# One of VectorE's shifted arrays moved in halves to GpSimd in an attention-plus-feed-forward kernel

## The chip, the cores and the metric

The kernel runs on one core of a Trainium2 chip. The time is the device time of one execution in microseconds (us). The kernel before took 769.64 us, the median of three runs (769.48 to 770.63). The engines of the core are TensorE (PE in the profile), VectorE (DVE), ScalarE (ACT), GpSimd (POOL) and SyncE (SP, which here only issues transfers).

## The reference

For one sequence of 2048 rows and 512 columns, attention with 32 heads of 16 columns and a gated feed-forward block of width 1792 are computed from the same x, and mixed by a gate per row.

```python
qkv = (x @ wqkv).reshape(B, S, 3, H, Dh).transpose(2, 0, 3, 1, 4)     # H = 32, Dh = 16
scores = einsum("bhqd,bhkd->bhqk", q, k) * Dh ** -0.5
a = (softmax(scores) @ v).transpose(0, 2, 1, 3).reshape(B, S, D) @ wo
b = (silu(x @ w_gate) * (x @ w_up)) @ w_down
g = sigmoid((x * gate_w).sum(-1))
out = g * a + (1 - g) * b
```

The exponentials are the large part: 32 heads x 2048 x 2048 of them.

## The kernel before, in words

The attention is cut into 32 units: a block of 512 queries (four of them) and a group of four heads (eight of them). A unit has 16 key tiles of 128 keys. A key tile of a unit, called n in the code, is four blocks of 128 keys x 512 queries, one per head. TensorE computes a block of scores into PSUM, something takes the exponential of it into SBUF, and TensorE multiplies it with the values into `o_ps`, where a unit's 16 key tiles are summed. `pv` (line 902) emits that product: one call is a "piece" of four matmuls, one per head, which run side by side on the 32-column groups of the array.

Exponentials are taken in two ways.

- **On ScalarE.** `emit_pair` (line 704) computes two blocks into `s_t` (two buffers), and one `Exp` over 128x1024 writes `e_t`. A key tile takes two of them, and then one piece of `pv`.
- **On VectorE.** `emit_d` (line 774) computes a single block into `d_t` (one of three PSUM banks). VectorE reads it out of PSUM with a multiply and an add into 16-bit integers, which read as bfloat16 are a rough power of two. Four such reads fill one array of 128x2048, called y, for the whole key tile. Then the rough exponential is mended in one of two ways, picked per key tile by `quad` (line 1469) and kept in `groups`:
  - `groups[n] == 4`: three arrays more, each y plus a constant (`copy`, line 817, `SHIFTS` 25, 56 and 94). All four go to TensorE, which adds them up: four pieces of `pv`.
  - `groups[n] == 2`: two arrays of y's bits (`bits`, line 825) and a product of y with one of them (`product`, line 834): two pieces of `pv`.

The arrays live in seven homes of 128x2048 (`home`, line 762), of which the seventh lies in `wd_t` or `kaug`.

Nothing is ordered by the hardware's own choice. The program is written in one pass, and a planner decides in Python, while the kernel is built, what each engine does next. `Plan` (line 289) has a clock for TensorE, ScalarE and VectorE, and each emitted instruction moves its engine's clock by a cost that is written in the code: 0.6 for a read of PSUM or a 128x2048 shift on VectorE, `MUL_US` 1.135 for the product, `ACT_US` 0.9167 for an exponential, 0.217 for a piece. The instructions of an engine are chained in that order by `ordered` (line 152), so the order is fixed once the kernel is built; the hardware adds only the waits.

What the change touches:

- `fill_dve` (line 854) writes VectorE's instructions as long as VectorE's clock is behind TensorE's. It chooses between `vops` (shifts, bits and products that wait for their turn), `d_wait` (reads of `d_t` that are due) and `owed` (all other VectorE work, with due times, put there by `later`, line 309).
- `m_free` (line 361) says when one of the three banks is free again: VectorE's clock plus 0.2. `emit_d` says when a `d_t` can be read: TensorE's clock plus 0.28 (line 807).
- `v_unit` (line 1444) decides whether VectorE may take one more key tile from ScalarE, from the work that it has already and from the clocks. So a lighter VectorE takes more key tiles.
- `quad` picks the form with four pieces when few homes are free or when TensorE has had idle time to spare (`spare`), or when `EAGER` says so. Before, `EAGER` is always false.

The feed-forward block's matmuls (`gu`, `ops`, `dps`) and the projections are cut into pieces too and laid by a pacer between the attention's. GpSimd writes constants in the first 12 us and does nothing after. A helper records each operation, so the profile shows most VectorE work under line 176, ScalarE's under 167 and matmuls under 164; the tiles' names tell them apart.

Of the kernel before, what the change touches and what calls it, by code (L numbers as in the profile page):

```python
# [79 lines left out]
def kernel(  # L80
# [37 lines left out]
    NV = 4  # L118
# [58 lines left out]

    vec = Ordered(nc.vector)
    queue = Ordered(nc.sync)


    xT = big.tile([P, DC, S], BF16, name="xT")
# [104 lines left out]


    class Plan:
        pe = dve = act = 0.0  # L290
        mode = last = None
        seq = 0
        slot = -1
# [8 lines left out]
    def spend(mode, mms, ready=0.0):  # L302
# [3 lines left out]
        plan.pe = max(plan.pe + (FLIP if mode != plan.mode else 0.0), ready) + (0.226 if mode == "F" else 0.217) * mms  # L306
        plan.mode = mode

    def later(cost, f, ready=None, key=None):
# [13 lines left out]

    def pay(i=0):
        ready, cost, f, c, key = owed.pop(i)
        spend_v(cost, ready, key)
# [33 lines left out]

    def m_free(ps, t):
        i = [h is ps for h in held].index(True)
        banks[i], held[i] = t + 0.2, None

    def emit_piece(c):
        mms, f = c.pieces[c.i][:2]
# [407 lines left out]
    def emit_d(i, rows=32, riding=False):  # L774
        if not vcur:
            n = v_take()
            waiting[n] = [NV, None, take_home()]
            vcur.update(n=n, left=list(range(NV)), y=None)
            y_live[0] += 1
        n, left, cur = vcur["n"], vcur["left"], waiting[vcur["n"]]  # L780
        left.remove(i)
        end = []
        d_t = m_tile("d_t", end if riding else None)
        score(d_t[:, :], 4 * n + i, rows)
        if not left:
            vcur.clear()

        def first():
            if cur[1] is None:
                cur[1] = home(*cur[2])  # L790
            h, y = cur[1]
            vec.tensor_scalar(out=y[:, i * QBW:(i + 1) * QBW], in0=d_t[:, :], scalar1=EXP_A, scalar2=EXP_B[groups[n]],
                              op0=ALU.mult, op1=ALU.add)
            m_free(d_t, plan.dve)
            cur[0] -= 1
            if cur[0]:
                return
# [12 lines left out]
    copies = {}  # L810
    part = {}

    def ready(n, k, h, c):
        copies[n, k] = (c.bitcast(BF16), h)
        vready.append((plan.dve + 0.3, n, k))

    def copy(n, k, i, y):
        h, c = home()
        vec.tensor_scalar(out=c, in0=y, scalar1=SHIFTS[k - 1], scalar2=None, op0=ALU.add)
        ready(n, k, h, c)  # L820
        if k == 3:
            drop(i, plan.dve + 0.2)
            y_live[0] -= 1

    def bits(n, k, y):
        h, c = home()
# [21 lines left out]

    def pay_v():
        cost, f, key, _, _ = vops.pop(0)  # L850
        spend_v(cost, 0.0, key)
        f()

    def fill_dve():

        while plan.dve <= plan.pe + 0.2:
            now = plan.dve
            due = [k for k, o in enumerate(owed) if o[0] <= now + 0.05]
            free = [k for k in due if owed[k][4] is None or owed[k][4] != plan.last]
            fit = bool(vops) and vops[0][3] // KT <= closed + AHEAD and c_ready() <= now  # L860
            if fit and vops[0][3] // KT < au and vops[0][2] != plan.last:
                pay_v()
            elif d_wait and d_wait[0][2] // KT < au and d_wait[0][0] <= now + 0.05:
                pay_d()
            elif free:
                pay(free[0])
            elif d_wait and d_wait[0][0] <= now + 0.05:
                pay_d()
            elif fit and vops[0][2] != plan.last:
                pay_v()  # L870
            elif due:
                pay(due[0])
            elif fit:
                pay_v()
            elif d_wait or owed or vops and vops[0][3] // KT <= closed + AHEAD:
                t = min([w[0] for w in d_wait] + [o[0] for o in owed[:1]]
                        + [c_ready()] * bool(vops and vops[0][3] // KT <= closed + AHEAD))
                if t > plan.pe:
                    break
                plan.dve = max(plan.dve, t)  # L880
                plan.last = None
            else:
                break
# [18 lines left out]
    def pv(n, k=None, most=QBW):  # L902

        un = n // KT
        c0 = cut.pop("done", 0)
        c1 = min(QBW, c0 + most)
        cols = slice(c0, c1)
        if un not in o_of:
            while un and un - 1 not in osbs:
                pay()  # L910
            plan.pe = max(plan.pe, o_end[0])
            o_of[un] = ps_o.tile([P, QBW], F32, tag="o", name="o_ps")
        if v_of(n) is not None:
# [12 lines left out]
        share = (c1 - c0) / QBW  # L926
        if c1 < QBW:
            cut.update(item=(n,) if k is None else (n, k), done=c1)
            spend("C", share, 0.0 if k is not None else max(e_end[b] for b in range(4 * n, 4 * n + 4)))
# [11 lines left out]
        spend("C", share, 0.0 if k is not None else max(e_end.pop(b, 0.0) for b in range(4 * n, 4 * n + 4)))  # L941
# [192 lines left out]

    plan.act = plan.pe
    plan.dve = plan.pe + 3.9


    pace = Pacer()
# [277 lines left out]
    def next_pv():  # L1417
        flush_act()
        while not pv_list(None):
            if d_wait:  # L1420
                pay_d()
            elif vops and c_ready() < 1e9:
                pay_v()
            elif owed:
                pay()
            else:
                lone_d()
        emit_pv(pv_list(None)[0])
# [45 lines left out]
            return False  # L1474
        return True
    FREE4 = 2
    EAGER = lambda q, b: False
    GQL = lambda: []
    back = [0]

    def want_d():
# [60 lines left out]
        at_ += not half  # L1542
        forward()
    flush_act()
    while closed < UNITS or vops or vcur:
        fill_dve()
        while owed and owed[0][0] <= plan.pe:
            pay()
        if plan.slot < SLOTS + 1:
            begin(plan.slot + 1)  # L1550
            pace.credit = max(pace.credit, 2.0)
        if vcur:
            lone_d()
            continue
        c = side(2.0)
        if not pv_list(plan.pe) and c is not None:
            put_piece(c)
            continue
        if closed == UNITS - 1 and pv_left(closed) <= 2 and not a_ps[2:]:
            tail_ready()  # L1560
            tail(3)
        next_pv()
# [6 lines left out]
            f()  # L1569
    while owed:  # L1570
        pay()
    assert not vops and not vready and not vcur and not d_wait and not copies and au == closed == UNITS


    assert not at
# [59 lines left out]
```

## Time and profile before

| what | value |
|---|---|
| median of three runs | 769.64 us (769.48 to 770.63) |
| the profiled execution | 769.63 us, of which its span is 767.9 us and 1.73 us lie around it |
| granted TensorE clock | 1.000 |
| busy: TensorE, VectorE, ScalarE, GpSimd | 733.1, 738.8, 752.5, 10.6 us |
| exponentials on ScalarE | 780, 728.3 us busy |
| key tiles on VectorE | 122 of 512: 44 with four pieces, 78 with two |

How to read it: the span runs from the first to the last instruction of that execution. Busy time is the union of an engine's instructions, so instructions that overlap on one engine count once; their mean duration can be longer than the distance from one start to the next. The last row is from the order of instructions in the built program: 488 blocks `d_t`, 288 shifts or bits over 128x2048, 78 products over 128x2048.

### The profile page before, as it was taken

To read this page: it belongs to the slowest core of one execution; us is meant where nothing else is said; L and a number is where in the kernel's file an instruction comes from. 1 tells how busy PE (TensorE), PEld (TensorE's weight loads), DVE (VectorE), ACT (ScalarE), POOL (GpSimd) and SP (SyncE) were. 2 spreads that over 40 slices of the span, in tenths; PEclk is the share of its full clock that TensorE was granted. 3 is DMA by queue.
4 is the path that set the end of the run, shared out by engine and by line. 5 is a ranking of instruction groups with operands and counts; after the bars stand their busy time and mean duration, and the time that the engine had idled before them with its cause. 6 is when DMAs were issued, how large, how long until landed. Compare 5 with 4: busy or idle time off the path is not lost.

```text
span 767.9 us, 22047 instructions
## 1 busy us (share of the span) xinstructions
PE 733.1 (95%) x9044; PEld 221.6 (29%) x9045; DVE 738.8 (96%) x1213; ACT 752.5 (98%) x849; POOL 10.6 (1%) x25
## 2 busy tenths in 40 slices
PE   8999999999999999999999999999999999999997
PEld 3323222222222222223322222223222322222222
DVE  6889999999999999999999999999999999999994
ACT  5999999999999999999999999999999999999996
POOL 5000000000000000000000000000000000000000
PEclk9999999999999999999999999999999999999999
DMA  8002304134200113220100230311000232100001
GB/s 192 2 5 50 73 15 85 31 107 101 57 19 13 32 24 78 60 52 22 37 26 12 49 84 20 75 34 41 20 12 26 60 77 59 31 16 16 16 28 35
DMA packets 91020, 34.38 MB, mean 45 GB/s; under 512 B 75488, under 2 KB 90472, under 8 KB 90920
## 3 DMA queue, kind: packets, MB, share of 16 engines
q1 hardware_dynamic: 89192, 32.66, 17.8%
q8 instruction: 70, 1.15, 0.6%
q10 hardware_dynamic: 1728, 0.33, 0.2%
q14 instruction: 30, 0.25, 0.1%
HBM read 21.55 MB, written 2.35 MB: 31 GB/s over the span
## 4 chain that ended last, share of the span: by engine, by line
ACT 32%; PE 30%; DVE 28%; issue 8%; DMA 1%; SPq 1%; DVEq 0%; ACTq 0%
ACT e_t L167 30%; DVE c_t L176 17%; PE s_t L164 10%; PE o_ps L164 8%; PE gu L164 6%; DVE kaug L176 3%; PE ops L164 3%; DVE mt L176 2%; DVE gs L176 2%; ACT th L167 1%; DVE on L176 1%; PE qp L164 1%; DVE osb L176 1%; PE warm L164 1%; SPq L176 1%
## 5 line engine op out<-in xcount | busy, mean ns | idle before, releaser
L167 ACT ACTIVATE e_t<-s_t 128x1024 bf16<-128x1024 f32 x780 | 728.3, 1105 | 1.3 <-PE s_t L164 0.7
L176 DVE TENSOR_SCALAR c_t<-d_t 128x512 uint16<-128x512 f32 x420 | 275.3, 681 | 2.2 <-PE d_t L164 2.0
L164 PE MATMUL s_t<-qx,kaug 32*128 32x512 bf16 (+1 forms) x1228 | 239.0, 384 | 16.1 <-ACT e_t L167 14.0
L164 PEld LDWEIGHTS <-kaug 32*128 32x128 bf16 (+1 forms) x2048 | 88.7, 91 | 321.8 <-issue 317.6
L164 PE MATMUL o_ps<-e_t,vaug 128*32 128x512 bf16 (+2 forms) x1608 | 154.2, 379 | 0.0
L176 DVE TENSOR_SCALAR c_t<-c_t 128x2048 uint16<-128x2048 uint16 x212 | 142.0, 683 | 1.7 <-PE o_ps L164 1.4
L164 PE MATMUL d_t<-qx,kaug 32*128 32x512 bf16 x404 | 131.9, 383 | 0.0
L164 PE MATMUL o_ps<-c_t,vaug 128*32 128x512 bf16 (+2 forms) x1244 | 111.3, 370 | 2.6 <-DVE osb L176 2.1
L164 PEld LDWEIGHTS <-vaug 128*32 128x32 bf16 x3048 | 68.8, 94 | 107.2 <-issue 95.2
L164 PE MATMUL gu<-xT,wg 128*32 128x512 bf16 x896 | 73.0, 384 | 0.0
L164 PE MATMUL gu<-xT,wu 128*32 128x512 bf16 x896 | 68.3, 382 | 0.2 <-DVE c_t L176 0.2
L176 DVE TENSOR_TENSOR c_t<-c_t 128x2048 bf16<-128x2048 bf16 x50 | 60.7, 1213 | 0.0
L164 PE MATMUL ops<-wd_t,mt 128*32 128x512 bf16 x672 | 57.5, 382 | 0.0
L164 PE MATMUL s_t<-q,kaug 32*128 32x512 bf16 (+1 forms) x196 | 38.2, 383 | 5.8 <-ACT e_t L167 5.4
L176 DVE TENSOR_SCALAR kaug<-d_t 128x512 uint16<-128x512 f32 x60 | 39.6, 680 | 0.0
L176 DVE SCALAR_TENSOR_TENSOR mt<-gs,gu 128x512 bf16<-128x512 bf16 x56 | 38.1, 680 | 1.5
L176 DVE SCALAR_TENSOR_TENSOR gs<-th,gu 128x512 bf16<-128x512 bf16 x56 | 38.0, 678 | 0.5 <-ACT th L167 0.5
L167 ACT ACTIVATE th<-gu 128x512 bf16<-128x512 f32 x56 | 37.7, 673 | 0.0
L164 PEld LDWEIGHTS <-mt 128*32 128x32 bf16 (+1 forms) x1037 | 24.5, 95 | 28.6 <-issue 22.0
L164 PEld LDWEIGHTS <-wu 128*32 128x32 bf16 x896 | 19.5, 95 | 25.4 <-issue 17.6
L164 PEld LDWEIGHTS <-wg 128*32 128x32 bf16 x896 | 17.8, 94 | 26.0 <-issue 23.2
L176 DVE TENSOR_SCALAR kaug<-c_t 128x2048 uint16<-128x2048 uint16 x33 | 22.5, 681 | 0.1
(141 smaller groups left out, 444.7 us busy)
## 6 DMA issues: line engine op xcount, KB each, us to landing
wg<-in_B_w_gate_dram SPq DMA_DIRECT2D x56, 128.0 KB
wu<-in_B_w_up_dram SPq DMA_DIRECT2D x56, 128.0 KB
on<-osb SPq DMA_DIRECT2D x120, 16.0 KB
rb<-rr SPq DMA_DIRECT2D x15, 128.0 KB
wd_t<-in_B_w_down_dram SPq DMA_DIRECT2D x7, 256.0 KB
qx<-qst SPq DMA_DIRECT2D x96, 16.0 KB
qx<-aq SPq DMA_DIRECT2D x96, 16.0 KB
out_dram<-o_t SPq DMA_DIRECT2D x12, 128.0 KB
```

The source lines that it names most:

```text
L164: return ordered(nc.tensor.matmul(*args, **kw))
L167: ordered(nc.scalar.activation(*args, **kw))
L176: return lambda *a, **kw: ordered(f(*a, **kw))
```

## The change

For at most one key tile at a time (`GQ = 1`), the third shifted array (constant 94) is no longer queued for VectorE. It is put into a list `gq`, and written in two halves of 128x1024. `g_now` begins a half on GpSimd when GpSimd's clock allows, a home is free, and at least `GNEED = 2` reads of PSUM are due on VectorE. The half has two operations (add 94, multiply by 1) and a wait on the last VectorE instruction written before it. From then until the half is planned to end, `plan.lock` holds VectorE back from everything that reads and writes only SBUF (`wide`, `locked`), and only reads of PSUM are written. If nothing else is to be done, VectorE takes a half itself (`g_dve`). Beside it, `m_free` goes from 0.2 to 0.14, a `d_t` may be read after 0.25 in place of 0.28, a shifted array has a due time of its own for `pv`, and `EAGER` becomes true when `gq` is empty and no more than four pairs are behind.

```diff
 def m_free(ps, t):
-    banks[i], held[i] = t + 0.2, None
+    banks[i], held[i] = t + 0.14, None
...
-                for k in range(1, 4):
+                todo[n] = 3
+                for k in range(1, 4 - (len(gq) < GQ)):
                     vops.append((0.6, lambda k=k: copy(n, k, h, y), ...))
+                if len(gq) < GQ:
+                    gq.append([n, h, y, [0, 1], None])
-        d_wait.append(((end[0] if end else plan.pe) + 0.28, first, n))
+        d_wait.append(((end[0] if end else plan.pe) + 0.25, first, n))
...
+    def g_half(engine, now):
...
+        half = left.pop(0)
+        cols = slice(half * GHALF, (half + 1) * GHALF)
+        before = last_of.get(nc.vector.engine)
+        ins = engine.tensor_scalar(out=c[1][:, cols], in0=y[:, cols], scalar1=SHIFTS[2], scalar2=1.0, op0=ALU.add, op1=ALU.mult)
+        if engine is gps:
+            if before is not None:
+                tc.add_manual_dep(ins.ins, before.name,
+                                  mybir.DependencyInfo(mybir.DependencyClass.Sync, mybir.DependencyReason.DATA),
+                                  reason="beside reads of PSUM")
+            t = plan.pool = plan.lock = max(plan.pool, now + 0.17) + 1.13
+        else:
+            t = plan.dve
...
+    def g_now(now):
+        while gq and gq[0][0] // KT <= closed + AHEAD and plan.pool <= now + 0.1 and (gq[0][4] is not None or min(c_free) <= now):
+            soon = sum(d[0] <= now + 0.05 + 0.6 * i for i, d in enumerate(d_wait)) + sum(o[0] <= now + 0.05 and not wide(o[1]) for o in owed)
+            if soon < GNEED:
+                return
+            g_half(gps, now)
+    GNEED = 2
+    def g_dve():
+        if gq[0][4] is None:
+            plan.dve = max(plan.dve, min(c_free))
+        spend_v(0.335, plan.lock)
+        g_half(vec, plan.dve)
...
 def fill_dve():
         while plan.dve <= plan.pe + 0.2:
             now = plan.dve
+            g_now(now)
+            shut = locked(now)
-            due = [k for k, o in enumerate(owed) if o[0] <= now + 0.05]
+            due = [k for k, o in enumerate(owed) if o[0] <= now + 0.05 and not (shut and wide(o[1]))]
-            fit = bool(vops) and vops[0][3] // KT <= closed + AHEAD and c_ready() <= now
+            fit = bool(vops) and not shut and vops[0][3] // KT <= closed + AHEAD and c_ready() <= now
...
+            elif gq and not shut and gq[0][0] // KT <= closed + AHEAD and (gq[0][4] is not None or min(c_free) <= now) and (len(gq) == GQ or not d_wait):
+                g_dve()
...
-    EAGER = lambda q, b: False
-    GQL = lambda: []
+    EAGER = lambda q, b: q == 0 and b <= 4
+    GQL = lambda: gq
```

In the built program the instructions of every engine stand in another order from early on, since each choice of the planner changes the next. The counts that differ:

| instructions | before | after |
|---|---|---|
| exponentials on ScalarE, 128x1024 | 780 | 772 |
| reads of `d_t`, VectorE | 488 | 504 |
| key tiles on VectorE with two pieces, with four | 78, 44 | 64, 62 |
| shifts and bits 128x2048, VectorE | 288 | 259 |
| products 128x2048, VectorE | 78 | 64 |
| halves 128x1024 on VectorE, on GpSimd | 0, 0 | 25, 85 |
| pieces of `pv` from VectorE's arrays, from `e_t` | 332, 390 | 376, 386 |
| filler pieces on TensorE | 3 | 1 |

More of the change, by code (lines that the diff above doesn't have):

```diff
@@ L179 @@
     queue = Ordered(nc.sync)
+    gps = Ordered(nc.gpsimd)
     xT = big.tile([P, DC, S], BF16, name="xT")
@@ L289 @@
     class Plan:
-        pe = dve = act = 0.0
+        pe = dve = act = pool = lock = 0.0
         mode = last = None
@@ L307, in spend, with wide, locked @@
         plan.mode = mode
+    def wide(cost):
+        return cost < 0.45
+    def locked(now):
+        return plan.lock > now + 0.03
     def later(cost, f, ready=None, key=None):
@@ L325, in pay @@
         ready, cost, f, c, key = owed.pop(i)
-        spend_v(cost, ready, key)
+        spend_v(cost, max(ready, plan.lock) if wide(cost) else ready, key)
         keep, plan.chain = plan.chain, None
@@ L804, in first, with usable @@
                 ready(n, 0, h, y)
-                for k in range(1, 4):
+                todo[n] = 3
+                for k in range(1, 4 - (len(gq) < GQ)):
                     vops.append((0.6, lambda k=k: copy(n, k, h, y), ("y", n) if k == 1 else None, n, True))
-        d_wait.append(((end[0] if end else plan.pe) + 0.28, first, n))
+                if len(gq) < GQ:
+                    gq.append([n, h, y, [0, 1], None])
+        d_wait.append(((end[0] if end else plan.pe) + 0.25, first, n))
+    def usable(t, n, k):
+        vready.append((t, n, k))
+        vready.sort(key=lambda v: v[0])
+        ready_at[n, k] = t
+    ready_at = {}
     waiting = {}
@@ L814, in ready @@
         copies[n, k] = (c.bitcast(BF16), h)
-        vready.append((plan.dve + 0.3, n, k))
+        usable(plan.dve + 0.3, n, k)
     def copy(n, k, i, y):
@@ L820, in copy, with copied @@
         ready(n, k, h, c)
-        if k == 3:
-            drop(i, plan.dve + 0.2)
-            y_live[0] -= 1
+        copied(n, i, plan.dve)
+    def copied(n, i, t):
+        todo[n] -= 1
+        if not todo[n]:
+            drop(i, t + 0.2)
+            y_live[0] -= 1
+    todo = {}
+    gq = []
+    GQ = 1
+    GHALF = NV * QBW // 2
+    def g_half(engine, now):
+        g = gq[0]
+        n, h, y, left, c = g
+        if c is None:
+            c = g[4] = home()
+        half = left.pop(0)
[10 more added lines that the diff above has]
+            t = plan.dve
+        if not left:
+            gq.pop(0)
+            usable(t + 0.3, n, 3)
+            copies[n, 3] = (c[1].bitcast(BF16), c[0])
+            copied(n, h, t)
+    def g_now(now):
[10 more added lines that the diff above has]
+        g_half(vec, plan.dve)
     def bits(n, k, y):
@@ L850, in pay_v @@
         cost, f, key, _, _ = vops.pop(0)
-        spend_v(cost, 0.0, key)
+        spend_v(cost, plan.lock, key)
         f()
@@ L874, in fill_dve @@
                 pay_v()
+            elif gq and not shut and gq[0][0] // KT <= closed + AHEAD and (gq[0][4] is not None or min(c_free) <= now) and (len(gq) == GQ or not d_wait):
+                g_dve()
             elif d_wait or owed or vops and vops[0][3] // KT <= closed + AHEAD:
-                t = min([w[0] for w in d_wait] + [o[0] for o in owed[:1]]
-                        + [c_ready()] * bool(vops and vops[0][3] // KT <= closed + AHEAD))
+                t = min([w[0] for w in d_wait] + [max(o[0], plan.lock if wide(o[1]) else 0.0) for o in owed[:1]]
+                        + [max(c_ready(), plan.lock)] * bool(vops and vops[0][3] // KT <= closed + AHEAD))
                 if t > plan.pe:
                     break
-                plan.dve = max(plan.dve, t)
+                plan.dve = max(plan.dve + 0.03, t)
                 plan.last = None
@@ L928, in pv @@
             cut.update(item=(n,) if k is None else (n, k), done=c1)
-            spend("C", share, 0.0 if k is not None else max(e_end[b] for b in range(4 * n, 4 * n + 4)))
+            spend("C", share, ready_at[n, k] if k is not None else max(e_end[b] for b in range(4 * n, 4 * n + 4)))
             return
@@ L940, in pv @@
             later(0.6, take_part, plan.pe + 0.47)
-        spend("C", share, 0.0 if k is not None else max(e_end.pop(b, 0.0) for b in range(4 * n, 4 * n + 4)))
+        spend("C", share, ready_at[n, k] if k is not None else max(e_end.pop(b, 0.0) for b in range(4 * n, 4 * n + 4)))
         if k is None:
@@ L1136 @@
     plan.dve = plan.pe + 3.9
+    plan.pool = 16.0
     pace = Pacer()
@@ L1423, in next_pv @@
                 pay_v()
+            elif gq and (gq[0][4] is not None or min(c_free) < 1e9):
+                g_dve()
             elif owed:
@@ L1544 @@
     flush_act()
-    while closed < UNITS or vops or vcur:
+    while closed < UNITS or vops or vcur or gq:
         fill_dve()
@@ L1571 @@
         pay()
-    assert not vops and not vready and not vcur and not d_wait and not copies and au == closed == UNITS
+    assert not vops and not gq and not vready and not vcur and not d_wait and not copies and au == closed == UNITS
     assert not at
```

## The prediction

> **What bounds the kernel now.** I began with busy time per engine, and then asked for the same by stretches, since an average hides which stage is full.
>
> ```profile
> PE 733.1 (95%) x9044; PEld 221.6 (29%) x9045; DVE 738.8 (96%) x1213; ACT 752.5 (98%) x849; POOL 10.6 (1%) x25
> ```
>
> ```profile
> 60.00:740.00 680.00, 655.52 (x8165) 194.37 (x8161) 673.62 (x1080) 679.63 (x768) 0.00 (x0) 1.00 0.18 44
> 700.00:740.00 40.00, 39.81 (x500) 10.92 (x492) 40.00 (x63) 40.00 (x45) 0.00 (x0) 1.00 0.08 26
> ```
>
> Columns of the second view: stretch, length, busy us (count) of PE, PEld, DVE, ACT, POOL, granted clock, DMA share, GB/s. From 60 to 740 us ScalarE is idle 0.4 us, VectorE 6.4, TensorE 24.5. ScalarE sets the time, VectorE is nearly as full, TensorE has some room. In the last 40 of these TensorE is busy 99.5% and ScalarE still never idle: a nearly full TensorE alone does not starve it.
>
> The waits say the same from the other side: the largest one of TensorE in that stretch is for ScalarE to give back a score buffer, and the waits for VectorE are small.
>
> ```profile
> PE s_t L164 <- ACT e_t L167: 18.7, 54, 0.7
> PE o_ps L164 <- DVE osb L176: 2.1, 5, 0.9
> PE o_ps L164 <- DVE c_t L176: 0.3, 1, 0.3
> ```
>
> So time is won only by fewer or shorter instructions on ScalarE, as long as the others keep up. Prices come from starts in the timeline, since neighbours overlap:
>
> ```profile
> 399.44 13.04 ACT L167 ACTIVATE e_t<-s_t 128x1024 bf16<-128x1024 f32 x14
> ...
> 402.72 1.28 DVE L176 TENSOR_SCALAR c_t<-d_t 128x512 uint16<-128x512 f32 x2
> 403.92 0.68 DVE L176 TENSOR_SCALAR c_t<-c_t 128x2048 uint16<-128x2048 uint16 x1
> 404.52 1.27 DVE L176 TENSOR_SCALAR c_t<-d_t 128x512 uint16<-128x512 f32 x2
> ...
> 407.52 1.21 DVE L176 TENSOR_TENSOR c_t<-c_t 128x2048 bf16<-128x2048 bf16 x1
> ...
> 408.65 1.28 DVE L176 TENSOR_SCALAR c_t<-d_t 128x512 uint16<-128x512 f32 x2
> ```
>
> Fourteen exponentials take 13.04 us, the last of them 1.105 (mean of the group): (13.04 - 1.105)/13 = 0.918 us from start to start. Two reads of PSUM: 403.92 - 402.72 = 1.20, so 0.60 each. A 128x2048 shift: 404.52 - 403.92 = 0.60. A product: 408.65 - 407.52 = 1.13.
>
> **The change part by part.** Counts are those of the built program.
>
> *ScalarE.* Eight exponentials fewer, 8 x 0.918 = 7.34 us; the 56 tanh stay. Nothing else stands on that engine, so all of it lies on the path as long as it is fed.
>
> *VectorE.* 16 more reads of PSUM, +9.6. 14 products fewer, -15.8. 29 shifts fewer, -17.4. 25 halves on VectorE: the trace has no 128x1024, but among the groups are 282 ns for a 128x512 16-bit pass (`aq<-qst`) and 683 for 128x2048, so 416 between, less the 0.08 by which neighbours overlap: 0.34 each, +8.5. Sum -15.1. Idle in the body becomes 6.4 + 15.1 - 7.3 = 14.2 us. That is what the new waits may use up for nothing.
>
> *TensorE.* 38 pieces more (44 more of VectorE's, 4 fewer of ScalarE's, 2 fillers fewer), 0.22 each by three that follow each other in the timeline (starts 409.19, 409.42, 409.63), +8.3. Eight pairs of scores fewer: between two pieces (starts 403.21 and 403.86) such a visit takes 0.65 less the first piece, 0.43, so -3.4. The 16 new blocks `d_t` run beside a pair's scores (both start at 403.54), 0. Sum +4.9, hidden in the idle time, which falls from 24.5 to 24.5 - 7.3 - 4.9 = 12.3.
>
> *GpSimd's half.* The trace has no such operation; its nearest rows are the constants at the start:
>
> ```profile
> 0.80 0.20 POOL L259 MEMSET ident<- 128x128 bf16 x1 [0.29 <-POOLq L1619]
> 0.94 0.32 POOL L263 MEMSET vaug<- 128x256 bf16 x1
> 1.28 0.29 POOL L260 TENSOR_SCALAR_AFFINE_SELECT ident<-ident 128x128 bf16<-128x128 bf16 x1
> ...
> 5.01 0.97 POOL L512 MEMSET q<- 128x1024 bf16 x1
> 5.90 0.63 POOL L273 MEMSET sbc_t<- 1x32 bf16 x4
> ```
>
> Writing 128x1024 takes 0.89 from start to start; that is the lower end. Reading as well costs 0.29 - 0.20 = 0.09 more at 128 elements. If that is paid once, a half takes 0.98; if per element, 8 x 0.09 more on 0.97, 1.69: the upper end. I take 1.10, nearer the lower end, because the 2048-element constant beside them takes 1.74, twice 0.87: elements stream, and reads can run beside writes. The signal to GpSimd adds about 0.08, as from TensorE to VectorE where a read that waited starts at 188.96 and its block ended at 188.88. Let T be signal plus half: 0.97 to 1.77, taken 1.18.
>
> *The wait.* The instruction that GpSimd waits for has ended when the half begins. What stands next on VectorE decides the cost, if both engines exclude each other for work inside SBUF, as the planner's lock assumes (the trace of before never has both at such work). In the built order 2 halves are followed by no read of PSUM, 39 by two, 25 by three, 19 by more, and then by SBUF work. At 0.60 a read, VectorE waits 2 x T + 39 x (T - 1.2) + 25 x (T - 1.8), each bracket at least 0. At T = 1.18 that is 2.4 us, under the 14.2 of idle. Idle time is not everywhere, so I charge 0.6, a quarter, to the path. At 1.77: 3.54 + 22.23 = 25.8, which exceeds the idle by 11.6. If they do not exclude each other, 0; a gain has no reason, since a wait adds no speed. Behind a waiting shift stand VectorE's next reads of PSUM; for the banks that they free waits TensorE, and for its scores ScalarE. Behind a waiting half stands only the next half. No transfer is added or taken away; those that SP issues follow their producers.
>
> The Trainium skill, "SBUF — State Buffer", section "Who interferes with whom", says the two engines hold a shared pair of ports as an exclusive lock for a whole instruction, but that a VectorE instruction with one SBUF input outside the two-port modes does not contend. No run here shows it; by it the reads of PSUM cover the half and the sum stays.
>
> *Due times.* 0.20 to 0.14 and 0.28 to 0.25 only choose the order; a wrong one makes an engine wait for the difference. The read at 188.96 begins 0.46 after its block at 188.50, and the block's slot is 0.22: 0.24 against 0.25, no loss. A bank is free 0.08 (end of the 0.68 after its 0.60 slot) plus a signal of 0.08 after the clock: 0.16 against 0.14, 0.02 early. Were each of the 504 reads waited for, 10 us, but TensorE is seldom next to a bank (the waits above): taken at 0, at best nothing gained. The longer waits of TensorE for GpSimd's arrays are for times with 0.3 of margin: 0.
>
> **Sum.** -7.34 + 0.6 = -6.7 on the profiled execution's 769.63 (span 767.9 and 1.73 around it): 762.9, said as 763.0. The median before is 769.64, so nothing is added for that.
>
> **Rivals.**
>
> *The half is long and VectorE becomes the bound* (slower). The idle is used up when 2T + 39(T - 1.2) = 14.2, at T = 1.49. The gain is gone at 41T - 46.8 = 21.5, T = 1.67, a half of 1.59 us. At 1.69 us it gives -7.34 + 11.6 = +4.2, 773.9. For it: the per-element reading of the select row, and that VectorE is 99% full already. Against: the streaming rows.
>
> The Trainium skill, "GPSIMD Engine Reference", section 3.1, speaks against the change: its measured best for a tight loop is 1.8 cycles an element at 1.2 GHz, an estimate of 1.54 us for a half. By that, T = 1.62, VectorE waits 19.6, and 5.4 of the gain goes: 767.7. The same section also has 1.03 cycles for one or two operations, 0.88 us, under the row above; no run here tells them apart yet.
>
> *TensorE becomes the bound.* If its 4.9 us more can't use the idle that lies before ScalarE's buffers, -7.34 + 4.9 = -2.4: 767.2. For it: 12.3 us of room is 1.8% of the body. Against: the last 40 us above.
>
> *It doesn't do what it says*, in that the cover is none: that the halves stay on VectorE is out, since 85 of 110 stand on GpSimd, but the reads of PSUM beside them might slow down. 170 reads (two a half) use up idle and gain at (14.2 + 7.34)/170 = 0.13 us each, on 0.60. If they stood still for the whole half, 85 x 1.10 - 14.2 - 7.34 = +72: 841. No row of before shows both engines at work inside SBUF; that the two use nothing in common for such a read is only what the lock of the code supposes. A small slowing, or the middle lengths of the half, give no change, about 769.6.
>
> **How the numbers follow.** What a measurement here can tell from no change is 0.2%, 1.5 us. The forecast, 760.5 to 765.5: 0.58. TensorE bound or a half near 1.5 us, 765.5 to 768.1: 0.13. Within 0.2%: 0.08. Slower: 0.21, of which 0.17 is the long half, most of it under 774 (its bound), and 0.04 reads that stand still. So faster 0.71, same 0.08, slower 0.21. The range goes from 760.5 (all 7.34, and 1.8 of a shorter end, of which there are 8.1 us after the last exponential at 734.73 + 25.05) to 774; about 0.12 is left out, 0.08 of it above.
>
> **What would show it.** Right: 772 exponentials, ScalarE's idle in the body still under 2 us; GpSimd's 85 halves near 1.1 us; VectorE's waits for GpSimd under 5 us in all; TensorE busy about 98% of the body. Wrong: halves of over 1.5 us and shifts of 128x2048 that take over 1 us or wait for POOL (the lock, priced too low); ScalarE idle before `e_t`, released by TensorE (TensorE bound).

## The result, and the profile after

The changed kernel takes 761.56 us (median of four runs, 761.05 to 761.86) against 769.56 before on the same chip: a ratio of 0.9895, 95% interval 0.988 to 0.991. That is 8.0 us saved; 6.6 had been forecast (763.0), and the range held it. The profiled execution is the fastest of the four, 761.05 us, with a span of 759.2.

Busy time per engine, from the page of the changed kernel:

```profile
PE 733.4 (97%) x9192; PEld 219.0 (29%) x9193; DVE 727.2 (96%) x1211; ACT 744.7 (98%) x841; POOL 99.3 (13%) x110
```

The same by stretch, and what TensorE waited for between 20 and 745 us:

```profile
60.00:735.00 675.00, 658.04 (x8322) 192.90 (x8320) 666.39 (x1084) 674.62 (x763) 85.56 (x82) 1.00 0.18 43
```

```profile
PE s_t L164 <- ACT e_t L167: 13.0, 45, 0.8
PE o_ps L164 <- DVE osb L176: 0.9, 2, 0.7
```

ScalarE still sets the time: 0.4 us idle in 675. TensorE waits 13.0 us for score buffers, where it waited 19.6 before in the same stretch. The two groups that carry the change:

```profile
L167 ACT ACTIVATE e_t<-s_t 128x1024 bf16<-128x1024 f32 x772 | 721.5, 1106 | 1.2 <-PE s_t L164 1.0
...
L176 POOL TENSOR_SCALAR c_t<-c_t 128x1024 uint16<-128x1024 uint16 x65 | 67.8, 1043 | 478.0 <-DVE c_t L176 328.0
```

All 85 halves on GpSimd take 1.043 to 1.046 us. How one of them stands beside VectorE, from the timeline of the changed kernel (start, length, engine):

```profile
328.71 1.22 DVE L176 TENSOR_TENSOR c_t<-c_t 128x2048 bf16<-128x2048 bf16 x1
...
329.85 0.68 DVE L176 SCALAR_TENSOR_TENSOR gs<-th,gu 128x512 bf16<-128x512 bf16 x1
...
330.01 1.04 POOL L176 TENSOR_SCALAR c_t<-c_t 128x1024 uint16<-128x1024 uint16 x1 [2.42 <-DVE c_t L176]
...
330.44 1.28 DVE L176 TENSOR_SCALAR kaug<-d_t 128x512 uint16<-128x512 f32 x2
...
331.64 0.68 DVE L176 TENSOR_SCALAR c_t<-c_t 128x2048 uint16<-128x2048 uint16 x1
```

The product ends at 329.93 and the half starts 0.08 later. Beside it stand only reads of PSUM, at their usual 0.68 and 1.28; the shift comes when the half is over. Added up over the trace, VectorE's instructions beside a half are longer than usual by 0.8 us in all, of which 0.67 are one small product of two SBUF inputs (`omg`, 0.84 in place of 0.17); no shift of 128x2048 is longer. The 132 reads of `d_t` that lie beside a half take 0.68 on the mean and 0.693 at most, as do the others.

Where the 8.58 us between the two profiled executions lie can be read from the first and the last group of exponentials, first of the kernel before, then of the changed one:

```profile
13.86 1.94 ACT L167 ACTIVATE e_t<-s_t 128x1024 bf16<-128x1024 f32 x2 [0.50 <-PE s_t L164]
...
734.73 25.05 ACT L167 ACTIVATE e_t<-s_t 128x1024 bf16<-128x1024 f32 x27
```

```profile
12.68 1.94 ACT L167 ACTIVATE e_t<-s_t 128x1024 bf16<-128x1024 f32 x2 [0.50 <-PE s_t L164]
...
723.97 26.80 ACT L167 ACTIVATE e_t<-s_t 128x1024 bf16<-128x1024 f32 x29
```

The first starts at 12.68 in place of 13.86 (1.18 less, since the first loads landed earlier; over the kernels below it lies anywhere from 12.6 to 13.8). From there to the end of the last it is 738.09 in place of 745.92, 7.83 less, of which 8 x 0.918 = 7.34 are the eight exponentials; the other 0.5 are fewer stops of ScalarE (7 of its exponentials are followed by idle time, where 11 were). After the last it is 8.48 in place of 8.12, 0.36 more. Around the span it is 0.07 more.

### The profile page after: what moved, and what is told of

Same layout as the page of the kernel before. It is cut to its first block, busy times and chain, and to the rows that moved or that the text cites. A ratio compares the mean times of both kernels' runs of the same rounds, so it can differ in the third digit from the quotient of the medians.

```text
span 759.2 us, 22471 instructions
## 1 busy us (share of the span) xinstructions
PE 733.4 (97%) x9192; PEld 219.0 (29%) x9193; DVE 727.2 (96%) x1211; ACT 744.7 (98%) x841; POOL 99.3 (13%) x110
## 3 DMA queue, kind: packets, MB, share of 16 engines
q8 instruction: 72, 1.18, 0.6%
## 4 chain that ended last, share of the span: by engine, by line
PE 37%; ACT 37%; DVE 17%; issue 8%; DMA 0%; SPq 0%; DVEq 0%; ACTq 0%
ACT e_t L167 35%; PE s_t L164 13%; DVE c_t L176 11%; PE o_ps L164 10%; PE gu L164 6%; PE ops L164 3%; ACT th L167 2%; DVE mt L176 2%; DVE kaug L176 2%; PE qp L164 1%; PE dps L164 1%; DVE gs L176 1%; PE kp L164 1%; PE vp L164 1%; PE warm L164 1%
## 5 line engine op out<-in xcount | busy, mean ns | idle before, releaser
L176 DVE TENSOR_SCALAR c_t<-d_t 128x512 uint16<-128x512 f32 x448 | 294.6, 683 | 5.9 <-PE d_t L164 4.9
L164 PEld LDWEIGHTS <-kaug 32*128 32x128 bf16 (+1 forms) x2048 | 85.2, 91 | 317.3 <-issue 313.9
L164 PE MATMUL d_t<-qx,kaug 32*128 32x512 bf16 x412 | 136.6, 383 | 0.1
L176 DVE TENSOR_SCALAR c_t<-c_t 128x2048 uint16<-128x2048 uint16 (+1 forms) x206 | 135.2, 666 | 1.2 <-PE o_ps L164 0.3
L176 POOL TENSOR_SCALAR c_t<-c_t 128x1024 uint16<-128x1024 uint16 x65 | 67.8, 1043 | 478.0 <-DVE c_t L176 328.0
L164 PE MATMUL o_ps<-c_t,vaug 128*32 128x512 bf16 (+2 forms) x1352 | 121.4, 373 | 1.1 <-DVE osb L176 0.9
L176 DVE TENSOR_TENSOR c_t<-c_t 128x2048 bf16<-128x2048 bf16 x42 | 51.1, 1216 | 0.0
L164 PEld LDWEIGHTS <-mt 128*32 128x32 bf16 (+1 forms) x1037 | 24.6, 95 | 29.1 <-issue 22.2
L176 DVE TENSOR_SCALAR kaug<-d_t 128x512 uint16<-128x512 f32 x48 | 31.7, 683 | 0.0
L176 DVE TENSOR_SCALAR kaug<-c_t 128x2048 uint16<-128x2048 uint16 (+1 forms) x45 | 28.8, 643 | 0.1
L164 PEld LDWEIGHTS <-wu 128*32 128x32 bf16 x896 | 19.9, 95 | 25.6 <-issue 16.5
```

Source lines behind the costliest of these rows:

```text
L164: return ordered(nc.tensor.matmul(*args, **kw))
L176: return lambda *a, **kw: ordered(f(*a, **kw))
```

## The experiments

Three groups of four kernels; each group ran on one chip with the kernel before (769.18, 769.03 and 769.08 us). The changed kernel was not run again beside them, so between groups the ratios are to be compared. All of them compute the whole reference. A row of the tables takes from the trace: the exponentials, the time from the start of the first to the end of the last, and the rest of that after 0.918 us for each exponential and 0.477 for each of the 56 tanh (start to start). The rest is what ScalarE lost, and 0.6 of two small operations that every kernel has.

### Which part of the change brings the gain

`due_only`: `GQ = 0` and `EAGER` always false.

```diff
-    GQ = 1
+    GQ = 0
...
-    EAGER = lambda q, b: q == 0 and b <= 4
+    EAGER = lambda q, b: False
```

> No half goes to GpSimd and the form with four pieces is preferred no more than before; only the due times differ from before (0.14, 0.25, a due time for each shifted array). The built program has 778 exponentials on ScalarE against 780. Theory A (time follows the exponentials on ScalarE, 0.918 us each): 2 x 0.918 = 1.8 us under before, about 767.8. Theory B (the due times are what brought the gain, GpSimd nothing): about 762. Theory C (TensorE sets the time; 723 pieces of products against 722, one filler more): no change, 769.6.

`due_eager`: `GQ = 0` alone.

> No half goes to GpSimd, but the due times and the preference for four pieces stay. 776 exponentials; VectorE has 20 products and 352 shifts; TensorE has 844 pieces of products against 722, +122 x 0.22 = 26.8 us, less 3 fillers (0.7) and 4 pairs (1.7): +24.4 on 24.5 us of idle in the body, which also shrinks by 3.7. Theory A: 4 x 0.918 = 3.7 us under before, 765.9. Theory B: about 762. Theory C: TensorE lacks about 4 us, so the gain is gone and the time is 769 to 771, with ScalarE idle before its exponentials.

`pool_old_due`: GpSimd stays, the old due times.

```diff
-    banks[i], held[i] = t + 0.14, None
+    banks[i], held[i] = t + 0.2, None
...
-        d_wait.append(((end[0] if end else plan.pe) + 0.25, first, n))
+        d_wait.append(((end[0] if end else plan.pe) + 0.28, first, n))
```

> GpSimd's halves and the preference stay, the two old due times (0.20 and 0.28) come back. 776 exponentials, 81 halves on GpSimd. Theory A: 3.7 us under before, 765.9; so the due times are worth the other 4 exponentials although they move no work. Theory B: no gain, 769.6. If only GpSimd counts and the planner's exponentials do not: 761.6 as the changed kernel.

`pool_no_eager`: `EAGER` always false, all else as changed.

> GpSimd's halves and the due times stay, the preference for four pieces is off. 776 exponentials, 63 halves on GpSimd, 716 pieces of products (762 in the changed kernel). Theory A: 765.9. Theory C (fewer pieces are better): under 762, as TensorE has 46 x 0.22 = 10 us less to do than in the changed kernel.

`pool_only`: both of the last two edits together.

> Only GpSimd's halves: due times at 0.20 and 0.28 as before, no preference for four pieces. 776 exponentials, 65 halves on GpSimd, 11 on VectorE, 722 pieces of products as before. Theory A, with what the earlier runs left of it (time = exponentials x their mean slot, given the same end): 4 x 0.918 = 3.7 us under before, 765.5 beside 769.2. Rival (GpSimd is worth something only together with the due times or the preference): 768 to 769.5.

| kernel | median us, ratio to before (95%) | exponentials | first to last, us | rest | after the last |
|---|---|---|---|---|---|
| before | 769.2 | 780 | 745.92 | 3.2 | 8.12 |
| `due_only` | 769.43, 1.0002 (0.9994 to 1.0011) | 778 | 746.08 | 5.2 | 8.12 |
| `due_eager` | 768.94, 0.9997 (0.9988 to 1.0006) | 776 | 743.14 | 4.1 | 11.05 |
| `pool_only` | 770.61, 1.0019 (1.0009 to 1.0028) | 776 | 747.24 | 8.2 | 8.12 |
| `pool_old_due` | 766.18, 0.9959 (0.9947 to 0.9972) | 776 | 742.45 | 3.4 | 8.25 |
| `pool_no_eager` | 766.28, 0.9961 (0.9949 to 0.9974) | 776 | 743.54 | 4.5 | 8.12 |
| changed | 761.56, 0.9895 (0.988 to 0.991) | 772 | 738.09 | 2.7 | 8.48 |

Without GpSimd nothing is gained, so theory B falls. Theory A holds to 0.4 us for `pool_old_due` and `pool_no_eager`; the latter also answers theory C, since with 46 pieces fewer than the changed kernel it is slower than that, not under 762. Theory A does not hold for the kernels without GpSimd: fewer exponentials in the program are a gain only if VectorE and TensorE can do what replaces them. Where that showed:

In `due_only` VectorE has no relief and one more key tile; by stretch it is 99.4% busy, and ScalarE idles 1.3 us where it idled 0.4:

```profile
60.00:740.00 680.00, 656.75 (x8160) 195.42 (x8152) 676.03 (x1086) 678.71 (x766) 0.00 (x0) 1.00 0.18 44
```

In `due_eager` VectorE has room, but TensorE has 122 pieces more than before. Theory C was right that the gain goes (768.94, just under its 769 to 771) and wrong in the place: ScalarE's timeline shows no wait in the body but one at the end.

```profile
734.54 21.23 ACT L167 ACTIVATE e_t<-s_t 128x1024 bf16<-128x1024 f32 x23
759.25 0.69 ACT L167 ACTIVATE osb<-o_ps,tiny 128x512 bf16<-128x512 f32 x1 [3.48 <-PE o_ps L164]
```

The last exponential ends at 755.77, and the last unit's sum is ready 3.48 us later, 2.9 more than before. Before that sum TensorE does 56 matmuls of the feed-forward block that had been put off:

```profile
754.70 3.19 PE L164 MATMUL ops<-wd_t,mt 128*32 128x512 bf16 x56
```

`pool_only` missed theory A (765.5) by 5 us; the rival's 768 to 769.5 is nearer, and missed by 1.1. One hole accounts for the 5 us: ScalarE's timeline, and TensorE's just before.

```profile
313.73 3.78 ACT L167 ACTIVATE e_t<-s_t 128x1024 bf16<-128x1024 f32 x4 [5.95 <-PE d_t L164]
```

```profile
309.07 0.40 PE L164 MATMUL o_ps<-kaug,vaug 128*32 128x512 bf16 x4 [0.80 <-DVE kaug L176]
310.21 2.49 PE L164 MATMUL o_ps<-c_t,vaug 128*32 128x512 bf16 x16 [0.73 <-DVE c_t L176]
```

TensorE takes VectorE's arrays one after another as they are written, and no scores in between; then the granted clock is 0.5 from 310.05 on for 3.41 us, which shows in the mean of the stretch around it (0.83 in the third column from the right):

```profile
305.00:315.00 10.00, 8.06 (x83) 2.04 (x75) 8.33 (x15) 4.05 (x6) 0.00 (x0) 0.83 0.14 34
```

Taking the 5.95 us away gives an estimate of 764.7. Why the planner wrote such an order there was not tried; it is no property of GpSimd, which is idle at that place.

So GpSimd's halves are needed, and the due times and the preference for four pieces are worth about 4.6 us each beside them (766.18 and 766.28 against 761.56). Without GpSimd the due times bring nothing, and neither do both together; the preference alone was not run. The halves alone bring nothing either, through a hole in one order of the planner. Each kernel here is one such order, so whether it has a hole is in part chance; the two kernels at 766 have none (rest 3.4 and 4.5), and of their 4.6 us 3.7 are the four exponentials that they have more.

### The lock, and how long a half may be

`twice`: each half on GpSimd is written two times, unknown to the planner, in the same order.

```diff
+            ordered(engine.tensor_scalar(out=c[1][:, cols], in0=y[:, cols], scalar1=SHIFTS[2], scalar2=1.0, op0=ALU.add, op1=ALU.mult))
             t = plan.pool = plan.lock = max(plan.pool, now + 0.17) + 1.13
```

> Each half on GpSimd is written twice, one right after the other, and the planner knows nothing of it: same order, GpSimd 2.09 us a half. Theory A (both engines exclude each other inside SBUF): T = 2.27, VectorE waits 2 x 2.27 + 39 x 1.07 + 25 x 0.47 = 58 us, of which its 8.6 us of idle in the body take a part: 761.6 + 49 = 811, and shifts beside a half start late or last up to 1.7 us. Rival (no exclusion; a half only comes later to TensorE): second halves come 1.04 us late on 55 key tiles, some of it covered by the 0.3 of margin: 762 to 790, and shifts of 128x2048 stay at 0.68 beside GpSimd.

`no_lock`: the halves go whenever they can.

```diff
-    GNEED = 2
+    GNEED = 0
...
-            t = plan.pool = plan.lock = max(plan.pool, now + 0.17) + 1.13
+            t = plan.pool = max(plan.pool, now + 0.17) + 1.13
```

> Halves go to GpSimd whenever a home is free, and the planner no longer keeps VectorE from work inside SBUF beside them. 770 exponentials on ScalarE, 138 halves on GpSimd, of which 63 are followed by no read of PSUM, 34 by one, 30 by two, 11 by more. Theory A: T = 1.22, VectorE waits 63 x 1.22 + 34 x 0.62 + 30 x 0.02 = 99 us, on some 10 of idle: about 845, slower than before. Rival (no exclusion): two exponentials fewer than the changed kernel, 759.8.

`one_op`: add 94 alone, same order.

```diff
-        ins = engine.tensor_scalar(..., scalar1=SHIFTS[2], scalar2=1.0, op0=ALU.add, op1=ALU.mult)
+        ins = engine.tensor_scalar(..., scalar1=SHIFTS[2], scalar2=None, op0=ALU.add)
```

> The shifted half is written with one operation (add 94) on both engines in place of two; the order of instructions is that of the changed kernel. Theory A: GpSimd's half has the same length (1.04 us in the changed kernel), time 761.6. Rival: the form with one operation is slower on GpSimd; then VectorE waits as in the prediction's sum, 2T + 39(T - 1.2) + 25(T - 1.8) with T the half plus 0.18: a half of 1.6 us gives 26.2 us of waiting on 8.6 of idle in the body, about 779; one of 2.1 us about 810.

`forms`: four spellings in turn, all with two operations.

```diff
+        form = ((SHIFTS[2], 1.0, ALU.add, ALU.mult), (SHIFTS[2], 0.0, ALU.add, ALU.add),
+                (1.0, SHIFTS[2], ALU.mult, ALU.add), (SHIFTS[2], 0.0, ALU.add, ALU.max))[forms[0] % 4]
+        forms[0] += 1
...
```

> The changed kernel with four spellings of the same half in turn, all with two operations: add 94 then multiply by 1; add 94 then add 0; multiply by 1 then add 94; add 94 then maximum with 0. Same order of instructions. If any second operation is what makes the half short, all four take 1.04 us and the time is 761.6. If it is the pair add and multiply alone, the other 40 to 60 halves take about 2.8 us as with one operation and the time is 785 to 805.

`whole`: the third array in one instruction.

```diff
-                    gq.append([n, h, y, [0, 1], None])
+                    gq.append([n, h, y, [0], None])
...
-    GHALF = NV * QBW // 2
+    GHALF = NV * QBW
...
-            t = plan.pool = plan.lock = max(plan.pool, now + 0.17) + 1.13
+            t = plan.pool = plan.lock = max(plan.pool, now + 0.17) + 2.0
...
-        spend_v(0.335, plan.lock)
+        spend_v(0.6, plan.lock)
```

> The third shifted array goes to GpSimd whole (128x2048) in place of two halves; the planner's length is 2.00 in place of 1.13, everything else stays. 772 exponentials, 59 arrays on GpSimd, none on VectorE; behind 4 of them stand fewer than three reads of PSUM, behind 26 three, behind 29 more. A whole array is taken at 1.04 + 0.87 (the difference of a 2048 and a 1024 constant) = 1.9, T = 2.1: VectorE waits at most 4 x 0.9 + 26 x 0.3 = 11 us. Theory A: 761.6 plus what of the 11 us is not hidden, 761 to 765. Rival (halves are needed to fit beside two reads): over 769.

| kernel | median us, ratio to before (95%) | half on GpSimd, us | VectorE longer, us | GpSimd longer, us | rest |
|---|---|---|---|---|---|
| changed | 761.56, 0.9895 (0.988 to 0.991) | 1.04 | 0.8 | 0 | 2.7 |
| `twice` | 801.30, 1.0416 (1.0401 to 1.0431) | 2 x 1.05 | 29.1 | 19.9 | 42.6 |
| `no_lock` | 788.12, 1.0244 (1.0231 to 1.0257) | 1.05 | 34.0 | 28.7 | 30.5 |
| `one_op` | 815.41, 1.0598 (1.0578 to 1.0618) | 2.77 | 24.0 | 10.7 | 54.2 |
| `forms` | 822.44, 1.0695 (1.0671 to 1.0719) | 1.04 and 3.63 | 5.1 | 1.9 | 61.8 |
| `whole` | 769.18, 1.0003 (0.9995 to 1.0012) | 1.90 (2048) | 5.8 | 0 | 10.7 |

"Longer" is what instructions that lie beside each other on the two engines took above their usual length, added up over the trace.

The exclusion is real, and it goes both ways. In the timeline of `no_lock`:

```profile
100.67 0.68 DVE L176 TENSOR_SCALAR c_t<-c_t 128x2048 uint16<-128x2048 uint16 x1
...
100.83 1.42 POOL L176 TENSOR_SCALAR c_t<-c_t 128x1024 uint16<-128x1024 uint16 x1 [0.74 <-DVE c_t L176]
...
102.63 1.05 POOL L176 TENSOR_SCALAR c_t<-c_t 128x1024 uint16<-128x1024 uint16 x1 [0.38 <-DVE c_t L176]
...
103.07 1.16 DVE L176 TENSOR_SCALAR wd_t<-c_t 128x2048 uint16<-128x2048 uint16 x1
```

The shift that began first keeps its 0.68 and the half takes 1.42; the shift that began second takes 1.16. It ends at 104.23, so it ran from 103.55, 0.13 before the half's end at 103.68; the 51 shifts of `no_lock` that waited for a half all ran on 0.14 before its end. The reads of PSUM keep their length beside halves in every run. The rule of the page "SBUF — State Buffer" of the Trainium skill (section "Who interferes with whom"), an exclusive lock that goes to whoever starts first, agrees with these four lines. The prediction cites it for a whole instruction; measured, the lock comes free 0.14 before the half's recorded end.

The prediction's sum for the wait, which reckons no half ever has to wait, expected 58 us in `twice` and 99 in `no_lock`; VectorE alone waited 29.1 and 34.0. In `twice` the two engines together come to 49.0, and the sum with T less the 0.13 gives 49.5, an agreement found afterwards and not tested further; in `no_lock` they come to 62.7, well under it, and why was not followed up. The times came out at 801 and 788 in place of 811 and 845: right in direction, too high in size. TensorE waits as well: in `twice` 17.3 us of its idle time before `o_ps`, from 20 to 750 us, end with an array of GpSimd's, and none in the changed kernel.

`one_op` shows that the spelling decides. The same half, the same bytes, 2.77 us in place of 1.04. And its lock is not held for the whole instruction:

```profile
101.90 2.77 POOL L176 TENSOR_SCALAR c_t<-c_t 128x1024 uint16<-128x1024 uint16 x1 [9.98 <-DVE ge L176]
...
102.86 0.68 DVE L176 TENSOR_SCALAR c_t<-c_t 128x2048 uint16<-128x2048 uint16 x1
...
104.10 1.12 DVE L176 TENSOR_SCALAR wd_t<-c_t 128x2048 uint16<-128x2048 uint16 x1
```

A shift 0.96 after the half's start runs freely in its midst; one at 2.20 waits for its end. Over the trace, shifts that come up to 0.61 after a half's start wait until about 0.9 (later where the half itself was held up), those from 0.93 to 1.71 do not wait, though the later ones of them make the half longer, and those from 1.75 on wait for its end (one at 1.82 did not, in a half that another instruction of VectorE's had already held up). The kernel takes 815 us; the prediction's sum with T = 2.77 + 0.18 gives 103 us of waiting and 856 us, too much, since VectorE's instructions are longer by 24.0 only. TensorE's idle time before `o_ps` that ends with an array of GpSimd's is 27.9 us here, up to 745 us.

`forms` settles what the second operation must be. Four halves of its timeline: add and multiply, add and add, multiply and add, add and maximum.

```profile
101.19 1.04 POOL L176 TENSOR_SCALAR c_t<-c_t 128x1024 uint16<-128x1024 uint16 x1 [9.98 <-DVE ge L176]
104.15 3.64 POOL L176 TENSOR_SCALAR c_t<-c_t 128x1024 uint16<-128x1024 uint16 x1 [1.92 <-DVE wd_t L176]
109.17 1.04 POOL L176 TENSOR_SCALAR wd_t<-c_t 128x1024 uint16<-128x1024 uint16 x1 [1.37 <-DVE c_t L176]
116.27 3.63 POOL L176 TENSOR_SCALAR wd_t<-c_t 128x1024 uint16<-128x1024 uint16 x1 [6.06 <-DVE c_t L176]
```

All 50 halves with a multiply and an add, in either order, take 1.04 (one of them 1.55, beside VectorE); all 35 others take 3.62 or more. The 785 to 805 us expected were reckoned with 2.8 for these; with 3.63 it is 822. So two operations are no merit by themselves; the pair of multiply and add is.

`whole` was expected at 761 to 765 and gave no change. That is the number of its rival (over 769), but the rival's reason, that a whole array does not fit beside two reads, is not shown: the array takes 1.90 as estimated, and the lock makes VectorE's instructions 5.8 us longer in all, 1.4 of them one operation on 128x16. As in `pool_only`, one hole carries most of it; here TensorE waits for GpSimd first:

```profile
309.19 0.40 PE L164 MATMUL o_ps<-c_t,vaug 128*32 128x512 bf16 x4 [1.35 <-POOL c_t L176]
```

ScalarE then idles 5.8 us and the granted clock is 0.5 from 311.89 on. A whole array is ready at once, where halves can be finished by VectorE (25 were). Whether halves would have spared this hole, or another order of the planner, stays open.

### Two settings that the planner is sensitive to

`bank_010`: a bank is planned to be free at 0.10. `lead_75`: the margin for one more key tile on VectorE.

```diff
-    banks[i], held[i] = t + 0.14, None
+    banks[i], held[i] = t + 0.10, None
```

> The changed kernel with the bank's due time at 0.10 in place of 0.14. 768 exponentials, 100 halves on GpSimd, 10 on VectorE. Theory A: 4 x 0.918 under the changed kernel, 757.9. Rival: a bank is free only 0.16 after the clock (the prediction's sum), so TensorE waits up to 0.06 at each of 512 blocks; with 12 us of TensorE's idle in the changed kernel's body against at most 31 us, the time is 760 to 765 and the slot of an exponential is longer than 0.918.

```diff
-    LEAD, LAST = 8.0, 6.0
+    LEAD, LAST = 7.5, 5.0
```

> The changed kernel with the margin for taking one more key tile onto VectorE at 7.5 in place of 8.0, and 5.0 in place of 6.0 for the last unit. 770 exponentials, 91 halves on GpSimd. Theory A: 2 x 0.918 under the changed kernel, 759.7 (beside 769.5 before). Rival (VectorE's arrays come too late at a unit's end, as its margin is smaller): 761.5 to 764, with ScalarE idle or a longer end after the last exponential.

`bank_010` took 767.11 us, ratio 0.9967 (0.9954 to 0.998): 768 exponentials, the fewest, and slower than the changed kernel. Both theories missed; the rival also reckoned with 12 us of idle time of TensorE, where the changed kernel's trace has 17.0. Its rest is 11.0 us, and after the last exponential it takes 1.9 us more than the changed kernel. TensorE's timeline:

```profile
120.20 0.62 PE L164 MATMUL o_ps<-c_t,vaug 128*32 128x512 bf16 x4 [1.28 <-DVE osb L176]
120.58 0.66 PE L164 MATMUL o_ps<-wd_t,vaug 128*32 128x512 bf16 x4
```

Groups of matmuls that take 0.39 elsewhere take 0.62 to 0.66: the granted clock is 0.5 from 120.11 on for 3.41 us, after 1.28 us without a matmul. It falls so at 328.3 and 625.3 too, and around the three, ScalarE idles 3.19, 1.46 and 0.65 us. Why it fell at the latter two is not seen, since the largest gap there was 0.68. The falls differ between executions: two of the seven have a mean clock of 0.999 and take 764.85 and 765.03 us, the other five 0.993 or 0.994 and 767.05 to 767.76. So the falls are worth an estimated 2.5 us; what keeps the other two above the changed kernel is open, as no trace of them was kept.

`lead_75` took 760.74 us, ratio 0.9892 (0.9878 to 0.9905), first to last 736.49, rest 2.9. Theory A's 759.7 was not reached: of the 1.8 us that two exponentials save, 0.8 return at the end, in the place that the rival named:

```profile
724.07 25.19 ACT L167 ACTIVATE e_t<-s_t 128x1024 bf16<-128x1024 f32 x27
750.96 0.69 ACT L167 ACTIVATE osb<-o_ps,tiny 128x512 bf16<-128x512 f32 x1 [1.69 <-PE o_ps L164]
```

The wait for the last unit's sum is 1.69 us here and 0.89 in the changed kernel. Its interval and the changed kernel's overlap, so it is not shown to be faster.

## Why the prediction was right, point by point

- **ScalarE sets the time, 8 x 0.918 = 7.34.** Right: 7.83 between the first and the last exponential, of which 7.34 are theirs. The experiments add weight to the condition that the others keep up, for which the sum had no term: where the planner's order left a hole, the rest rose from 2.7 to 8.2 (`pool_only`) and 11.0 (`bank_010`). That the changed kernel has no such hole was not foreseen, and is luck as far as the prediction goes.
- **The wait, charged with 0.6.** The step is right, and its size about so: 0.8 us of longer instructions, of which 0.67 lie in one small product that the sum did not have, while ScalarE's idle time in the body stayed at 0.4. T was taken as 1.18; signal and half measure 0.08 to 0.18 and 1.04, so 1.12 to 1.22. But the lock is given back 0.13 before the half's end, and in the tight cases (two reads) the next instruction inside SBUF starts 0.93 to 1.04 after the half's start, when 0.91 have been needed. It fits with 0.02 to 0.13 to spare.
- **GpSimd's half, 0.89 to 1.69, taken as 1.10.** It is 1.04. Reading runs beside writing, as the streaming rows said: 128x2048 in `whole` takes 1.90, so 0.85 for each further 1024 and 0.19 once.
- **The rival with the long half** was one spelling away: at 2.77 us (`one_op`) the kernel takes 815. The sum gave the threshold, a half of 1.59 us; no run was made near it, so its place was not tested. Of the two figures of the page "GPSIMD Engine Reference" of the Trainium skill (section 3.1), the trace agrees with 1.03 cycles an element (by the page an estimate of 0.88 us for a half; measured are 1.04, and 0.85 for each further 1024) for a multiply and an add, not with 1.8. The prediction cites that figure for one or two operations; for others than this pair it does not hold, since one add alone took 2.77, and add with add 3.64.
- **The rival with TensorE.** It did not become the bound in the changed kernel, where ScalarE is idle 0.4 us of the body. With 122 pieces more, in `due_eager`, its late work cost 2.9 us at the end.
- **The rival with reads that slow down.** Ruled out: in no run does a read of `d_t` beside a half take more than 0.693 us, the most that one without a half takes.
- **VectorE -15.1, idle in the body 14.2.** Mis-sized: busy time fell by 11.6, and the idle time from 60 to 735 us is 8.6. VectorE stands idle before 119 instructions, where it did before 90, and at each such stop the 0.08 by which neighbours overlap counts as busy again (2.3 us); 0.7 more is `omg`. It waits for `d_t` 4.9 us where it waited 2.0. Since the halves cost nearly nothing, the difference did not come into the time.
- **TensorE +4.9, idle 12.3.** Mis-sized: busy time rose by 0.3, and the idle time is 17.0. The pieces may well have cost what was counted: TensorE stands idle before 105 matmuls, where it did before 137, and a last matmul counts its whole 0.38 as busy where a followed one counts 0.22, so 32 stops fewer take 5.1 us out of the busy time.
- **Due times at 0.** As a step of the changed kernel, wrong: they are worth 4.6 us beside GpSimd (`pool_old_due`). With their old values the planner keeps four exponentials more. They had been priced for the waits that they could add, not for the key tiles that they let the planner move. Those were in the sum all the same, as part of the eight exponentials.
- **The sum, 6.7 saved, 8.6 measured in the profiled executions:** 1.18 are the earlier first load, which is chance (the first exponential starts anywhere from 12.6 to 13.9 us in these kernels), 0.5 fewer stops of ScalarE, 0.6 the charge for the wait, which did not come, less 0.4 at the end and 0.1 around the span.

## What to carry to other kernels

An engine that is nearly idle can take work from a full one even if they exclude each other, when the work is cut into pieces that fit beside instructions that do not need what they share; count, in the built order, how many such instructions stand behind each piece, and compare with its measured length. Before that, measure the operation itself in more than one spelling: here the same half took 1.04, 2.77 or 3.63 us. In a kernel whose order is planned, the count of instructions on the bounding engine predicts the time only as far as the other engines keep up: look for the one or two holes, and for the clock in them, before blaming the edit.

## What the runs showed of the hardware that was not expected

- On GpSimd, `tensor_scalar` over 128x1024 16-bit integers takes 1.04 us with a multiply and an add in either order, 2.77 with one add, 3.63 with add and add or add and maximum.
- The one-add form excludes VectorE's shifts for about its first 0.9 and from about 1.75 on, and not between (`one_op`).
- A granted clock of 0.5 for 3.41 us followed a gap of TensorE of 1.28 us (`bank_010`) and two gaps of 0.80 and 0.73 within 2 us (`pool_only`), but single gaps of 1.54 (`twice`) and 2.87 us (`one_op`) left it at 1.0, so the length of the gap does not decide. Within a trace the falls begin whole multiples of 3.413 us apart (61.0 and 87.0 of them in `bank_010`, 66.0 in `one_op`). Cut into such stretches from 20 us on, and without the last 20, in `pool_only`, `whole`, `twice`, `one_op`, `forms` and `bank_010`, each of the ten in which TensorE was busy under 52% was followed by a fall, and of those in which it was busy for over 55% only two were (64 and 76%, before the latter two falls of `bank_010`), which stay unexplained.
- A product of two SBUF inputs of only 128x16 took 0.84 us, in place of 0.17, where a half on GpSimd lay beside it (`omg` in the changed kernel), and 0.175 where it fell into the free middle of one with a single add (`one_op`).
